# A transformer block on one core: the front before K reordered (single x loads, a shared PSUM bank, the scale through a row of ones), and the shift section and the s store moved

## The chip, the cores and the metric

The kernel runs on one core of a Trainium2 chip. The metric is the device time of one execution in microseconds (us); for one core that is the core's own time. All times of stages below come from one profiled execution and count from the start of its span.

## The reference, cut to what matters

Two batches of 256 tokens, width 1152 (9 chunks of 128), 2 heads, an MLP of width 4608, all in bf16. The first part, which the change concerns, is the adaptive LayerNorm before K, Q and V:

```
mod = (silu(c) @ w_mod).reshape(B, 6, 1, D)
shift_a, scale_a, gate_a, shift_m, scale_m, gate_m = [mod[:, i] for i in range(6)]
h = layernorm(x) * (1 + scale_a) + shift_a
q, k, v = split(h @ wqkv)
attn = softmax(q @ k^T * Dh**-0.5)
x = x + gate_a * ((attn @ v) @ wo)
h2 = layernorm(x) * (1 + scale_m) + shift_m
return x + gate_m * (gelu(h2 @ w_fc1) @ w_fc2)
```

## The kernel before, in words

Tokens lie as four tiles of 128 (tiles 0, 1 are batch 0; tiles 2, 3 batch 1). The stages run in this order: LayerNorm 1 and K, then Q, scores and softmax, V, attention times V, the output projection with LayerNorm 2, and the two MLP products. On each engine the instructions run in the order in which the program is written: a loop at the end of the kernel ties every instruction to the one before it on its engine. Waits between engines are put in by the tile framework, which also hands out the banks: `aux` tiles have two PSUM banks, `acc` tiles six. A transposed block `pt`, a scale group `pm`, and the shift section `pn` are `aux` tiles; the K sums `pk` are `acc` tiles.

The front, line by line:

- L83 to L85 load c (on ScalarE's queue) and x (on SP's queue, one load per batch). L103 to L110 put w_scale_a and w_k on the same queue in four groups of chunks (0-1, 2-3, 4-5, 6-8): a group's scale columns, then its rows of w_k, the first six column tiles of K (KM1 = 6) at first and the last three afterwards. w_shift_a, w_q and the s_b loads (L476) follow on that queue.
- L169 are matmuls on zeros that keep TensorE running while nothing has landed. L172, L173 transpose c and form s = silu(c), kept as sT.
- `stats_piece` (L185) takes the statistics of a third of a tile on VectorE and closes them after the third; tile 1's statistics are taken on ScalarE (`act_stats`, L200) and closed by three small VectorE operations (`act_stats_finish`, L205). `sqrt1` (L216) is ScalarE's square root, `recip1` (L219) VectorE's reciprocal, `norm1` (L226) normalizes columns of a tile; the first 512 columns (CUT) of each tile come first, the rest after L381.
- `scale_group` (L241) forms 1 + scale_a of a group: 9 small matmuls per chunk with weights from w_scale_a, and a copy that adds one (L254 on VectorE, L256 on ScalarE).
- `transpose_x` (L260) transposes chunks of normalized tiles on TensorE into a bank, and `modulate` (L267) scales them into hT0 on VectorE ("d") or ScalarE ("a"). `modulated_transpose` (L275) does both for one chunk of all four tiles.
- `k_step` (L282) adds one chunk's product to the six K sums, for a range of tokens. L329 to L405 write out by hand how these pieces interleave. The six sums are evacuated (L407), `k_panel` (L312) makes the last three column tiles of K one by one, and `vec_section` (L412) forms the shift with small matmuls and one VectorE transpose.
- L434 to L442 add the shift: hT = hT0 + shift_a, on VectorE and ScalarE. Q (L493) reads hT.
- L388, L389 write s by rows to DRAM: one VectorE transpose and four DMA issues on POOL's queue. s_b (L476) reads it back, for scale_m's products on VectorE (L469).

Of the kernel before, what the change touches and what calls it, by code (L numbers as in the profile page):

```python
# [8 lines left out]
FP32 = mybir.dt.float32  # L9
BF16 = mybir.dt.bfloat16  # L10
ACT = mybir.ActivationFunctionType
# [8 lines left out]
def kernel(  # L20
# [11 lines left out]
    nc = tc.nc  # L32
    B, N, D = x.shape
# [3 lines left out]
    P = 128  # L37
    T = B * N
    NT = T // P
    TPB = N // P  # L40
    KD = D // P
# [3 lines left out]
    NPD = D // PW  # L45
# [6 lines left out]
    const = ctx.enter_context(tc.tile_pool(name="const", bufs=1))  # L52
# [18 lines left out]
    wmod_v = w_mod.rearrange("(k p) n -> p k n", p=P)  # L71
# [3 lines left out]
    S_SHIFT_A, S_SCALE_A, S_GATE_A, S_SHIFT_M, S_SCALE_M, S_GATE_M = range(6)  # L75
# [5 lines left out]
    x_sb = act.tile([P, NT, D], BF16, name="x_sb", tag="x_in")  # L81
    c_sb = act.tile([B * KD, P], BF16, name="c_sb")
    nc.scalar.dma_start(c_sb[:], c_v)  # L83
    for b in range(B):
        nc.sync.dma_start(x_sb[:, b * TPB:(b + 1) * TPB, :], x_v[:, b, :, :])  # L85

    zeros = const.tile([P, T], BF16, name="zeros")
    nc.vector.memset(zeros[:], 0.0)
    ident = const.tile([P, P], BF16, name="ident")
    make_identity(nc, ident[:])  # L90
    eps_t = const.tile([P, 1], FP32, name="eps_t")
    nc.vector.memset(eps_t[:], LN_EPS)  # L92
    one_t = const.tile([P, 1], FP32, name="one_t")
    nc.vector.memset(one_t[:], 1.0)
    SW = 32
    sT = act.tile([P, KD, SW], BF16, name="sT")
    nc.gpsimd.memset(sT[:], 0.0)
# [5 lines left out]
    for k0, k1 in KGROUPS:  # L103
        nc.sync.dma_start(
            w_scale_a[:, :, k0 * P:k1 * P],
            wmod_v[:, :, S_SCALE_A * D + k0 * P:S_SCALE_A * D + k1 * P],
        )
# [92 lines left out]
    def act_stats(f, dst):  # L200
        nc.scalar.activation(
            xns[T_ACT][:], x_sb[:, T_ACT, :], f, bias=pivot, scale=-1.0, accum_out=dst[:],
        )
# [12 lines left out]
    def sqrt1(t):  # L216
        nc.scalar.activation(rstd1[:, t:t + 1], mv1[:, t, 1:2], ACT.Sqrt, bias=eps_t[:], scale=1.0)
# [20 lines left out]

    scale_a = act.tile([P, KD, B], FP32, name="scale_a")

    def scale_group(g):  # L241
        k0, k1 = KGROUPS[g]
        pm = aux_tile([P, k1 - k0, B], "pm")
        for j in range(k0, k1):
            for k in range(KD):
                nc.tensor.matmul(
                    pm[:, j - k0, :], w_scale_a[:, k, j * P:(j + 1) * P], sT[:, k, 0:B],
                    start=(k == 0), stop=(k == KD - 1),
                )

        def add_one(eng):
            dst = scale_a[:, k0:k1, :]
            if eng == "d":
                nc.vector.tensor_scalar_add(dst, pm[:], 1.0)  # L254
            else:
                nc.scalar.activation(dst, pm[:], ACT.Identity, bias=one_t[:])  # L256

        return add_one

    def transpose_x(ks, ts, pt=None, js=None):  # L260
        pt = aux_tile([P, len(ks), len(ts) * P], "pt", BF16) if pt is None else pt
        for i, k in enumerate(ks):
            for j, t in enumerate(ts) if js is None else zip(js, ts):
                nc.tensor.transpose(pt[:, i, j * P:(j + 1) * P], xns[t][:, k * P:(k + 1) * P], ident[:])
        return pt

    def modulate(pt, i, k, t0, j0, w, eng):  # L267
        b = t0 // TPB
        dst, src, sc = hT0[:, k, t0 * P:t0 * P + w], pt[:, i, j0:j0 + w], scale_a[:, k, b:b + 1]
        if eng == "d":  # L270
            nc.vector.tensor_scalar_mul(dst, src, sc)
        else:
            nc.scalar.mul(dst, src, sc)
# [8 lines left out]
    def k_step(k, c0=0, c1=T):  # L282
        for m in range(KM1):
            if k == 0 and c0 == 0:
                pk[m] = acc_tile([P, T], "pk")
            nc.tensor.matmul(  # L286
                pk[m][:, c0:c1], w_k[:, k, m * P:(m + 1) * P], hT0[:, k, c0:c1],
                start=(k == 0 and c0 == 0), stop=(k == KD - 1), skip_group_check=True,
            )
# [19 lines left out]
    def k_evac(m):  # L309
        evac(kT[:, m, :], pk[m][:])  # L310

    def k_panel(m):  # L312
        pk[m] = acc_tile([P, T], "pk")
        for k in range(KD):
# [12 lines left out]

    CUT = 4 * P
    warm(12, pwarm)  # L329
    act_stats(ACT.Identity, dsum)  # L330
    for j in range(NPD):
        stats_piece(0, j)
    sqrt1(0)
    act_stats(ACT.Square, dsq)
    stats_piece(2, 0)
    recip1(0)
    norm1(0, 0, CUT, "d")
    stats_piece(2, 1)
    pt_0 = transpose_x([0, 1], [0])
    warm(4, pwarm)  # L340
    act_stats_finish()
    sqrt1(T_ACT)
    stats_piece(2, 2, False)
    recip1(1)
    norm1(1, 0, CUT, "d")
    stats_aggregate(2)
    scale_group(0)("a")
    for k in range(2):
        modulate(pt_0, k, k, 0, 0, P, "a")
    warm(1, pwarm)  # L350
    pt_1 = transpose_x([0, 1], [1])
    for k in range(2):
        modulate(pt_1, k, k, 1, 0, P, "d")
    sqrt1(2)
    k_step(0, 0, P)
    k_step(1, 0, P)
    stats_piece(3, 0)
    recip1(2)
    norm1(2, 0, CUT, "d")
    k_step(0, P, N)  # L360
    k_step(1, P, N)
    stats_piece(3, 1)
    stats_piece(3, 2)
    pt_2 = transpose_x([0, 1], [2])
    for k in range(2):
        modulate(pt_2, k, k, 2, 0, P, "a")
    scale_group(1)("a")
    sqrt1(3)
    recip1(3)
    norm1(3, 0, CUT, "d")  # L370
    k_step(0, N, N + P)
    k_step(1, N, N + P)
    pt_3 = transpose_x([2, 3], [0, 1])
    for i, k in enumerate((2, 3)):
        modulate(pt_3, i, k, 0, 0, N, "a")
    pt_4 = transpose_x([0, 1], [3])
    for k in range(2):
        modulate(pt_4, k, k, 3, 0, P, "d")
    k_step(2, 0, N)
    k_step(3, 0, N)  # L380
    norm1(0, CUT, D, "d")  # L381
    norm1(1, CUT, D, "d")
    pt_5 = transpose_x([2, 3], [2, 3])
# [1 line left out]
        modulate(pt_5, i, k, 2, 0, N, "a")  # L385
    norm1(2, CUT, D, "d")
    norm1(3, CUT, D, "d")
    nc.vector.transpose(s_rows[:].rearrange("p k c -> p (k c)"), sT[:].rearrange("p k c -> p (k c)"))  # L388
    store_by_quadrant(s_dram[:].rearrange("b (k a r) -> a b k r", a=4, r=32), s_rows, B)  # L389
    k_step(0, N + P, T)  # L390
    k_step(1, N + P, T)
    scale_group(2)("d")
    k_step(2, N, T)
    modulated_transpose(4)
    k_step(3, N, T)
    modulated_transpose(5)
# [508 lines left out]
```

## Time and profile before, and how to read it

| what | us |
|---|---|
| median of 8 runs | 243.6 (243.49 to 244.08) |
| the profiled execution's own time | 243.94 |
| its span | 242.2 |
| x of batch 0, of batch 1 landed | 4.34, 5.8 |
| scale groups 0, 1, 2, 3 landed | 8.86, 11.92, 15.0, 19.0 |
| first k_step starts | 10.22 |
| k_step of chunk 2 starts | 14.13 |
| last piece of w_shift_a landed | 30.8 |
| shift section starts | 30.34 |
| Q starts | 33.51 |
| first MLP product starts | 97.4 |

In the tables by stretches the columns are: the stretch, its length, then busy time (and instructions) of TensorE's matmuls, its weight loads, VectorE, ScalarE and GpSimd, then the granted TensorE clock, the mean busy share of the 16 DMA engines, and GB/s. In a timeline, a line is start, duration, engine, source line, operation, output from input, shape and count; in brackets stands how long the engine had been idle before it and what ended that. Ends of matmuls are modelled, and a matmul that runs in a stream overlaps the next: the spacing of starts is the cost, not the duration. A landing time is the start of a load's issue plus the profile's time from issue to landing.

### The profile page before, as it was taken

The page shows a single profiled execution, that of the slowest core. Times are in us where ns is not written, and L with a number is a line of the kernel's source. Part 1 is how long each engine was busy: PE and PEld are TensorE (multiplying, and loading weights), DVE is VectorE, ACT ScalarE, POOL GpSimd, SP SyncE. Part 2 cuts the span into 40 slices and gives each one's busy share as a digit, 9 for nine tenths or more (in the row PEclk, how much of TensorE's full clock was granted, in tenths as well). Part 3 has the DMA queues.
Part 4 walks back from the last instruction along what each step waited for, and adds up shares of the span by engine and source line. Part 5 has one row for each costly group of instructions (what it writes and reads, how often), then busy time and mean ns, then how long its engine had stood idle before and what let it go on. Part 6 is the DMA issues. An engine that isn't in the chain of part 4 may idle for free.

```text
span 242.2 us, 4031 instructions
## 1 busy us (share of the span) xinstructions
PE 236.2 (98%) x1698; PEld 143.0 (59%) x1698; DVE 93.2 (38%) x207; ACT 70.4 (29%) x140; POOL 31.9 (13%) x48
## 2 busy tenths in 40 slices
PE   8899999999999999999999999999999999999994
PEld 2586454466566566888854444444656665665573
DVE  3762450665694676620000019999002000000001
ACT  6542250543736073782222233332000000000000
POOL 1022000000310617200000000000314111111111
PEclk9999999999999999999999999999999999999999
DMA  6999999999999999899999999997791000000000
GB/s 227 325 333 342 385 355 240 337 369 284 237 323 361 381 259 193 223 195 328 327 326 262 196 249 329 326 327 218 230 297 42 19 16 16 20 19 27 21 16 16
DMA packets 76989, 54.48 MB, mean 225 GB/s; under 512 B 26011, under 2 KB 72491, under 8 KB 76971
## 3 DMA queue, kind: packets, MB, share of 16 engines
q1 hardware_dynamic: 76240, 53.02, 78.0%
q0 software_dynamic: 704, 1.20, 1.6%
q8 instruction: 13, 0.21, 0.4%
q14 instruction: 5, 0.04, 0.1%
q10 hardware_dynamic: 27, 0.00, 0.0%
HBM read 46.90 MB, written 1.19 MB: 199 GB/s over the span
## 4 chain that ended last, share of the span: by engine, by line
PE 58%; ACT 2%; DMA 2%; issue 0%; DVE 0%; ACTq 0%; DVEq 0%
PE pacc L850 29%; PE pacc L786 29%; ACT hT L671 2%; DMA hT<-xn 2%; ACT xn L650 0%; ACT rstd L641 0%; DVE tmp L856 0%; DVE o_sb L858 0%; ACTq L671 0%; DVEq L856 0%
## 5 line engine op out<-in xcount | busy, mean ns | idle before, releaser
L786 PE MATMUL pacc<-hT,w_f 128*128 128x256 bf16 (+1 forms) x432 | 70.7, 326 | 0.3 <-ACT hT L671 0.2
L850 PE MATMUL pacc<-w_f,gT 128*128 128x384 bf16 (+2 forms) x468 | 70.5, 314 | 0.0
L850 PEld LDWEIGHTS <-gT 128*128 128x128 bf16 x468 | 44.4, 98 | 26.2
L786 PEld LDWEIGHTS <-w_f 128*128 128x128 bf16 x432 | 42.2, 98 | 28.3 <-issue 0.7
L469 DVE SCALAR_TENSOR_TENSOR late<-w_gate_mT,late 128x1152 bf16<-128x1152 bf16 x18 | 24.4, 1358 | 36.7 <-DMA w_gate_mT<-in_w_mod_dram 36.1
L856 DVE TENSOR_TENSOR tmp<-pacc,gate 128x384 f32<-128x384 f32 (+2 forms) x13 | 6.8, 526 | 62.2 <-PE pacc L850 50.4
L824 ACT ACTIVATE gT<-pacc 128x512 bf16<-128x512 f32 x24 | 14.3, 597 | 32.3 <-PE pacc L786 32.3
L469 DVE SCALAR_TENSOR_TENSOR s_spill<-w_scale_m,s_b 128x1152 bf16<-128x1152 bf16 x12 | 16.3, 1357 | 8.6 <-DMA w_scale_m<-in_w_mod_dram 8.3
L689 PE MATMUL pacc<-w_o,big 128*128 128x384 bf16 (+2 forms) x117 | 17.9, 314 | 0.0
L568 PE MATMUL pacc<-w_v,hT 128*128 128x384 bf16 x108 | 17.9, 326 | 0.0
L858 POOL TENSOR_TENSOR o_sb<-tmp,x 128x384 bf16<-128x384 f32 (+1 forms) x12 | 11.6, 973 | 47.1 <-DVE tmp L856 47.1
L689 PEld LDWEIGHTS <-big 128*128 128x128 bf16 x117 | 11.0, 98 | 6.8 <-ACT big L611 0.2
L568 PEld LDWEIGHTS <-hT 128*128 128x128 bf16 x108 | 10.4, 98 | 7.0 <-issue 0.2
L286 PE MATMUL pk<-big,w_k 128*128 128x128 bf16 (+2 forms) x102 | 13.4, 278 | 0.1
L695 POOL TENSOR_TENSOR x<-tmp,x_sb 128x384 f32<-128x384 f32 (+1 forms) x11 | 9.8, 889 | 17.4 <-DVE tmp L694 9.9
L495 PE MATMUL pacc<-hT,w_q 128*128 128x512 bf16 x54 | 11.8, 379 | 0.0
L324 POOL DMA_DIRECT2D gates_dram<-grow x4 | 2.1, 518 | 71.0 <-DVE grow L810 71.0
L802 ACT ACTIVATE gT<-pacc 128x512 bf16<-128x512 f32 x12 | 6.9, 595 | 10.2 <-PE pacc L786 10.2
L286 PEld LDWEIGHTS <-w_k 128*128 128x128 bf16 x102 | 7.8, 97 | 3.1 <-issue 0.2
L495 PEld LDWEIGHTS <-w_q 128*128 128x128 bf16 x54 | 5.3, 98 | 6.4
L694 DVE TENSOR_TENSOR tmp<-pacc,gate 128x384 f32<-128x384 f32 (+2 forms) x13 | 6.7, 522 | 5.4 <-PE pacc L689 5.2
L169 PE MATMUL pwarm<-zeros 128*128 128x512 bf16 x21 | 7.6, 515 | 1.2 <-DVE eps_t L92 1.2
(99 smaller groups left out, 159.6 us busy)
## 6 DMA issues: line engine op xcount, KB each, us to landing
w_f<-in_w_fc_dram SPq DMA_DIRECT2D x14, 864.0 KB, 10.8
w_f<-in_w_fc_dram SPq DMA_DIRECT2D x2, 2592.0 KB, 10.5
w_f<-in_w_fc_dram SPq DMA_DIRECT2D x2, 1728.0 KB, 14.2
w_shift_a<-in_w_mod_dram SPq DMA_DIRECT2D x3, 864.0 KB, 11.0
w_v<-in_wqkv_dram SPq DMA_DIRECT2D x3, 864.0 KB, 6.1
w_gate_a<-in_w_mod_dram SPq DMA_DIRECT2D x3, 864.0 KB, 9.2
w_o<-in_wo_dram SPq DMA_DIRECT2D x3, 864.0 KB, 6.4
w_shift_m<-in_w_mod_dram SPq DMA_DIRECT2D x3, 864.0 KB, 13.0
```

Source lines behind the costliest of these rows:

```text
L169: nc.tensor.matmul(dst[:], zeros[:, 0:P], zeros[:], start=True, stop=True)
L286: nc.tensor.matmul(pk[m][:, c0:c1], w_k[:, k, m * P:(m + 1) * P], hT0[:, k, c0:c1], start=(k == 0 and c0 == 0), stop=(k == KD - 1), skip_g ...
L469: nc.vector.scalar_tensor_tensor(spill, wT[:, j, :], 1.0, s_b[b], op0=ALU.mult, op1=ALU.mult, accum_out=dst(j, b),)
L495: nc.tensor.matmul(pq[m][:], w_q[:, k, m * P:(m + 1) * P], hT[:, k, :], start=(k == 0), stop=(k == KD - 1),)
L568: nc.tensor.matmul(pacc[:], hT[:, k, t * P:(t + 1) * P], w_v[:, k, pnl * PW:(pnl + 1) * PW], start=(k == 0), stop=(k == KD - 1),)
L689: nc.tensor.matmul(pacc[:], aT[:, k, t * P:(t + 1) * P], w_o[:, k, c0:c1], start=(k == ks[0]), stop=(k == ks[-1]),)
L695: (nc.vector if (t, i) in ((1, 2), (3, 3)) else nc.gpsimd).tensor_tensor(x1[:, t, c0:c1], tmp[:], x_sb[:, t, c0:c1], op=ALU.add)
L786: nc.tensor.matmul(dst, w_f1[m // KD][:, k, ml * P:(ml + 1) * P], hT[:, k, c0:c1], start=(k == 0), stop=(k == KD - 1),)
L802: nc.scalar.activation(gT[:, ms[0]:ms[-1] + 1, b * N:(b + 1) * N], pacc[:], ACT.Gelu_apprx_tanh)
L824: nc.scalar.activation(gT[:, m, :], pacc[:], ACT.Gelu_apprx_tanh)
L850: nc.tensor.matmul(pacc[:], gT[:, kk, t * P:(t + 1) * P], w_f2[j][:, r, c0 - n * PW:c0 - n * PW + cw], start=(kk == 0), stop=(kk == KF - 1),)
L858: (nc.vector if last else nc.gpsimd).tensor_tensor(o_sb[:], tmp[:], x1[:, t, c0:c0 + cw], op=ALU.add)
```

## The change

- x of batch 0 is loaded as two single tiles, batch 1 as before in one load.
- The constant one is now a row of 128 ones in bf16 on a single partition. A scale group starts with one matmul of that row by itself, which puts 1 into the bank; the 9 matmuls per chunk add to it, and the copy that follows adds nothing.
- For chunks 0, 1 of tile 0 and chunks 2, 3 of tiles 0, 1, VectorE scales straight with the scale in PSUM; ScalarE's copy to scale_a follows.
- Tile 1's and 2's chunks 0, 1 and the chunks 2, 3 of tiles 0, 1 are transposed into one bank (pt_1), eight blocks of 128 columns.
- VectorE's order changes: all three pieces of tile 2 and the first of tile 3 come ahead of tile 1's reciprocal and norm.
- `k_step` can do some of its six column tiles: chunk 3's step is split around tile 3's transposes, chunk 5's around scale group 3. Scale group 2 moves ahead of the k_steps of chunks 0, 1 for tile 3; its copy stays after them.
- The shift section moves into the last K tile: 5 of its 9 matmuls, the section, then 4.
- The s transpose and its four stores move behind chunk 8's scaling.

```diff
-    for b in range(B):
-        nc.sync.dma_start(x_sb[:, b * TPB:(b + 1) * TPB, :], x_v[:, b, :, :])
+    for l in range(TPB):
+        nc.sync.dma_start(x_sb[:, l, :], x_v[:, 0, l, :])
+    nc.sync.dma_start(x_sb[:, TPB:NT, :], x_v[:, 1, :, :])
...
+    def scale_group_matmuls(g):
         k0, k1 = KGROUPS[g]
         pm = aux_tile([P, k1 - k0, B], "pm")
+        nc.tensor.matmul(
+            pm[:].rearrange("p j b -> p (j b)"), ones_r[:, 0:P], ones_r[:, 0:(k1 - k0) * B], start=True, stop=False,
+            skip_group_check=True,
+        )
...
-                    start=(k == 0), stop=(k == KD - 1),
+                    start=False, stop=(k == KD - 1), skip_group_check=True,
...
-    act_stats(ACT.Identity, dsum)
     for j in range(NPD):
         stats_piece(0, j)
+    act_stats(ACT.Identity, dsum)
     sqrt1(0)
     act_stats(ACT.Square, dsq)
-    stats_piece(2, 0)
     recip1(0)
     norm1(0, 0, CUT, "d")
-    stats_piece(2, 1)
+    for j in range(NPD):
+        stats_piece(2, j)
     pt_0 = transpose_x([0, 1], [0])
     warm(4, pwarm)
     act_stats_finish()
     sqrt1(T_ACT)
-    stats_piece(2, 2, False)
+    sqrt1(2)
+    stats_piece(3, 0)
     recip1(1)
     norm1(1, 0, CUT, "d")
-    stats_aggregate(2)
-    scale_group(0)("a")
+    pm_0 = scale_group_matmuls(0)
     for k in range(2):
-        modulate(pt_0, k, k, 0, 0, P, "a")
-    warm(1, pwarm)
-    pt_1 = transpose_x([0, 1], [1])
+        nc.vector.tensor_scalar_mul(hT0[:, k, 0:P], pt_0[:, k, 0:P], pm_0[:, k, 0:1])
+    nc.scalar.copy(scale_a[:, 0:2, :], pm_0[:])
+    pt_1 = aux_tile([P, 1, 8 * P], "pt", BF16)
...
     for k in range(2):
-        modulate(pt_1, k, k, 1, 0, P, "d")
-    sqrt1(2)
+        transpose_into(pt_1, k, k, 1)
+    recip1(2)
+    norm1(2, 0, CUT, "d")
+    for k in range(2):
+        modulate(pt_1, 0, k, 1, k * P, P, "a")
     k_step(0, 0, P)
     k_step(1, 0, P)
-    stats_piece(3, 0)
-    recip1(2)
-    norm1(2, 0, CUT, "d")
-    k_step(0, P, N)
-    k_step(1, P, N)
     stats_piece(3, 1)
     stats_piece(3, 2)
-    pt_2 = transpose_x([0, 1], [2])
     for k in range(2):
-        modulate(pt_2, k, k, 2, 0, P, "a")
-    scale_group(1)("a")
+        transpose_into(pt_1, 6 + k, k, 2)
+    k_step(0, P, N)
+    for k in (2, 3):
+        for t in range(TPB):
+            transpose_into(pt_1, 2 * (k - 1) + t, k, t)
+    k_step(1, P, N)
+    for k in range(2):
+        modulate(pt_1, 0, k, 2, (6 + k) * P, P, "a")
     sqrt1(3)
+    k_step(0, N, N + P)
+    pm_1 = scale_group_matmuls(1)
     recip1(3)
     norm1(3, 0, CUT, "d")
-    k_step(0, N, N + P)
+    for k in (2, 3):
+        nc.vector.tensor_scalar_mul(
+            hT0[:, k, 0:N], pt_1[:, 0, 2 * (k - 1) * P:2 * k * P], pm_1[:, k - 2, 0:1]
+        )
+    nc.scalar.copy(scale_a[:, 2:4, :], pm_1[:])
     k_step(1, N, N + P)
-    pt_3 = transpose_x([2, 3], [0, 1])
-    for i, k in enumerate((2, 3)):
-        modulate(pt_3, i, k, 0, 0, N, "a")
+    k_step(2, 0, N)
+    k_step(3, 0, N, 0, 3)
     pt_4 = transpose_x([0, 1], [3])
     for k in range(2):
         modulate(pt_4, k, k, 3, 0, P, "d")
-    k_step(2, 0, N)
-    k_step(3, 0, N)
+    k_step(3, 0, N, 3, KM1)
...
-    nc.vector.transpose(s_rows[:].rearrange("p k c -> p (k c)"), sT[:].rearrange("p k c -> p (k c)"))
-    store_by_quadrant(s_dram[:].rearrange("b (k a r) -> a b k r", a=4, r=32), s_rows, B)
+    add2 = scale_group(2)
     k_step(0, N + P, T)
     k_step(1, N + P, T)
-    scale_group(2)("d")
+    add2("d")
...
     k_step(4)
+    k_step(5, m1=2)
     scale_group(3)("d")
     modulated_transpose(6)
-    k_step(5)
+    k_step(5, m0=2)
     modulated_transpose(7)
     k_step(6)
     modulated_transpose(8)
+    nc.vector.transpose(s_rows[:].rearrange("p k c -> p (k c)"), sT[:].rearrange("p k c -> p (k c)"))
+    store_by_quadrant(s_dram[:].rearrange("b (k a r) -> a b k r", a=4, r=32), s_rows, B)
...
     k_evac(7)
+    k_panel(8, 0, 5)
     shift_a = vec_section(sT, w_shift_a, "shift_a")
-    k_panel(8)
+    k_panel(8, 5)
```

More of the change, by code (lines that the diff above doesn't have):

```diff
@@ L92 @@
     nc.vector.memset(eps_t[:], LN_EPS)
-    one_t = const.tile([P, 1], FP32, name="one_t")
-    nc.vector.memset(one_t[:], 1.0)
+    ones_r = const.tile([1, P], BF16, name="ones_r")
+    nc.vector.memset(ones_r[:], 1.0)
     SW = 32
@@ L102, with load_scale_group @@
     w_k = wide_tile("w_k")
[L103 to L107, printed above, removed]
+    def load_scale_group(g, eng):
+        c0, c1 = KGROUPS[g][0] * P, KGROUPS[g][1] * P
+        eng.dma_start(w_scale_a[:, :, c0:c1], wmod_v[:, :, S_SCALE_A * D + c0:S_SCALE_A * D + c1])
+    for g, (k0, k1) in enumerate(KGROUPS):
+        load_scale_group(g, nc.sync)
         for k in range(k0, k1):
@@ L239 @@
     scale_a = act.tile([P, KD, B], FP32, name="scale_a")
-    def scale_group(g):
+    def scale_group_matmuls(g):
         k0, k1 = KGROUPS[g]
         pm = aux_tile([P, k1 - k0, B], "pm")
+        nc.tensor.matmul(
+            pm[:].rearrange("p j b -> p (j b)"), ones_r[:, 0:P], ones_r[:, 0:(k1 - k0) * B], start=True, stop=False,
+            skip_group_check=True,
+        )
         for j in range(k0, k1):
@@ L247, in scale_group, with scale_group_copy, copy_out @@
                     pm[:, j - k0, :], w_scale_a[:, k, j * P:(j + 1) * P], sT[:, k, 0:B],
-                    start=(k == 0), stop=(k == KD - 1),
+                    start=False, stop=(k == KD - 1), skip_group_check=True,
                 )
-        def add_one(eng):
+        return pm
+    def scale_group_copy(g, pm):
+        k0, k1 = KGROUPS[g]
+        def copy_out(eng):
             dst = scale_a[:, k0:k1, :]
             if eng == "d":
-                nc.vector.tensor_scalar_add(dst, pm[:], 1.0)
+                nc.vector.tensor_copy(dst, pm[:])
             else:
-                nc.scalar.activation(dst, pm[:], ACT.Identity, bias=one_t[:])
-        return add_one
+                nc.scalar.copy(dst, pm[:])
+        return copy_out
+    def scale_group(g):
+        return scale_group_copy(g, scale_group_matmuls(g))
     def transpose_x(ks, ts, pt=None, js=None):
@@ L280, with k_step @@
     pk = [None] * KD
-    def k_step(k, c0=0, c1=T):
-        for m in range(KM1):
+    def k_step(k, c0=0, c1=T, m0=0, m1=KM1):
+        for m in range(m0, m1):
             if k == 0 and c0 == 0:
@@ L310, in k_evac, with k_panel @@
         evac(kT[:, m, :], pk[m][:])
-    def k_panel(m):
-        pk[m] = acc_tile([P, T], "pk")
-        for k in range(KD):
+    def k_panel(m, ka=0, kb=KD):
+        if ka == 0:
+            pk[m] = acc_tile([P, T], "pk")
+        for k in range(ka, kb):
             nc.tensor.matmul(
@@ L342, with transpose_into @@
     sqrt1(T_ACT)
-    stats_piece(2, 2, False)
+    sqrt1(2)
+    stats_piece(3, 0)
     recip1(1)
     norm1(1, 0, CUT, "d")
-    stats_aggregate(2)
-    scale_group(0)("a")
+    pm_0 = scale_group_matmuls(0)
     for k in range(2):
-        modulate(pt_0, k, k, 0, 0, P, "a")
-    warm(1, pwarm)
-    pt_1 = transpose_x([0, 1], [1])
-    for k in range(2):
-        modulate(pt_1, k, k, 1, 0, P, "d")
-    sqrt1(2)
+        nc.vector.tensor_scalar_mul(hT0[:, k, 0:P], pt_0[:, k, 0:P], pm_0[:, k, 0:1])
+    nc.scalar.copy(scale_a[:, 0:2, :], pm_0[:])
+    pt_1 = aux_tile([P, 1, 8 * P], "pt", BF16)
+    def transpose_into(pt, slot, k, t):
+        nc.tensor.transpose(pt[:, 0, slot * P:(slot + 1) * P], xns[t][:, k * P:(k + 1) * P], ident[:])
+    for k in range(2):
+        transpose_into(pt_1, k, k, 1)
[3 more added lines that the diff above has]
+        modulate(pt_1, 0, k, 1, k * P, P, "a")
     k_step(0, 0, P)
     k_step(1, 0, P)
-    stats_piece(3, 0)
-    recip1(2)
-    norm1(2, 0, CUT, "d")
-    k_step(0, P, N)
-    k_step(1, P, N)
     stats_piece(3, 1)
     stats_piece(3, 2)
-    pt_2 = transpose_x([0, 1], [2])
     for k in range(2):
-        modulate(pt_2, k, k, 2, 0, P, "a")
-    scale_group(1)("a")
+        transpose_into(pt_1, 6 + k, k, 2)
[6 more added lines that the diff above has]
+        modulate(pt_1, 0, k, 2, (6 + k) * P, P, "a")
     sqrt1(3)
+    k_step(0, N, N + P)
+    pm_1 = scale_group_matmuls(1)
     recip1(3)
     norm1(3, 0, CUT, "d")
-    k_step(0, N, N + P)
+    for k in (2, 3):
[3 more added lines that the diff above has]
+    nc.scalar.copy(scale_a[:, 2:4, :], pm_1[:])
     k_step(1, N, N + P)
-    pt_3 = transpose_x([2, 3], [0, 1])
-    for i, k in enumerate((2, 3)):
-        modulate(pt_3, i, k, 0, 0, N, "a")
+    k_step(2, 0, N)
+    k_step(3, 0, N, 0, 3)
     pt_4 = transpose_x([0, 1], [3])
```

## The prediction

> **What bounds the kernel now.** I read the page first, then the chain that ended last, then the timeline of the first 34 us, since the change lies there.
>
> ```profile
> PE 236.2 (98%) x1698; PEld 143.0 (59%) x1698; DVE 93.2 (38%) x207; ACT 70.4 (29%) x140; POOL 31.9 (13%) x48
> ```
>
> TensorE is never free for long. The chain of waits, in order of time, ends in two stretches of nothing but matmuls:
>
> ```profile
> 98.87 69.59 PE pacc L786 x425
> 168.46 70.30 PE pacc L850 x468
> ```
>
> No TensorE wait of over 0.3 us stands between 14.13 us and 98.87 us, and what starts that last chain (LN2) is itself fed by TensorE. So a shift of the front reaches the end in full. The table by stretches says where the front has room:
>
> ```profile
> 8.86:10.22 1.36, 1.12 (x22) 0.72 (x23) 0.29 (x3) 0.68 (x3) 0.00 (x0) 1.00 1.15 321
> 10.22:14.13 3.91, 3.53 (x62) 2.97 (x62) 3.14 (x10) 2.04 (x8) 0.00 (x0) 1.00 1.13 320
> 14.13:33.51 19.38, 19.38 (x200) 11.83 (x198) 8.38 (x24) 6.29 (x15) 2.58 (x4) 1.00 1.07 360
> ```
>
> From 14.13 us on TensorE is dense. Before that the timeline has the steps:
>
> ```profile
> 4.98 1.24 ACT L201 ACTIVATE xn<-x_sb 128x1152 bf16<-128x1152 bf16 x1
> 6.21 0.28 ACT L217 ACTIVATE rstd<-mv,eps_t 128x1 f32<-128x1 f32 x1
> 8.86 0.60 PE L246 MATMUL pm<-sT,w_scale_a 128*128 128x2 bf16 x18 [0.42 <-DMA w_scale_a<-in_w_mod_dram]
> 9.50 0.26 ACT L256 ACTIVATE scale_a<-pm,one_t 128x4 f32<-128x4 f32 x1 [1.24 <-PE pm L246]
> 9.80 0.62 ACT L273 ACTIVATE big<-pt,scale_a 128x128 bf16<-128x128 bf16 x2
> 9.82 0.27 PE L264 MATMUL pt<-ident,xn 128*128 128x128 bf16 x2
> 10.22 1.50 PE L286 MATMUL pk<-big,w_k 128*128 128x128 bf16 x24
> 13.61 0.84 ACT L273 ACTIVATE big<-pt,scale_a 128x256 bf16<-128x256 bf16 x2 [0.42 <-PE pt L264]
> 14.13 1.47 PE L286 MATMUL pk<-big,w_k 128*128 128x256 bf16 x12
> ```
>
> k_step starts at 10.22 us. Its 36 narrow matmuls at 0.055, 8 transposes at 0.055 and 18 scale matmuls at 0.027 make 2.9 us of issue until 14.13, so about 1.0 us is waiting: that is all that the front could give.
>
> **What the skill says.** (1) "PSUM — Partial Sum Buffer", PSUM bank collisions raise a hardware error: two engines may not touch one bank and quadrant at once, so software orders them. The trace agrees: chunk 4's transposes run from 17.44 to 17.83, and its first scaling starts only at 17.86, though it reads the first two; and pt_1's transposes, placed in the bank of the first pm, start at 9.82, after ScalarE's last read of it at 9.76. (2) "TensorEngine Tiling (Array Packing)", Tiling Modes, Key Properties: changing the tiling mode drains TensorE. The trace agrees: before 64-row matmuls the weight load stood idle, and the first one comes 0.20 us after its forerunner (54.38 to 54.58) where 0.11 is the spacing, thus 0.09 more; the 18-row transpose at 3.02 is followed by a 128-row matmul at 3.14.
>
> ```profile
> 54.58 0.33 PEld L532 LDWEIGHTS <-big 64*128 64x128 bf16 x8 [0.21 <-issue]
> 30.34 0.98 PEld L417 LDWEIGHTS <-sT 128*32 128x32 bf16 x36 [0.42 <-issue]
> ```
>
> **The change, part by part.**
>
> *Loads.* SP issues three loads of x for two, at 0.43 us each, so the first scale group is issued 0.43 later. DMA share is 0.8 to 1.1 from 2.5 us on, so a load queued 0.43 later may still be served at once when its turn comes; I expect its landing (8.86) to move by 0 to 0.43. Tile 0 may land some 0.7 earlier than 4.34. That gives nothing: the square root of tile 0 (6.21) stands in ScalarE's queue behind the statistics of tile 1 (4.98), which stand behind a table load; the order of these two is not changed.
>
> *VectorE's new order.* Spacings from the trace, start to start: reciprocal 0.20, half norm 0.32, a statistics piece 0.47 (0.58 before its aggregate), aggregate 0.16, 128-wide scaling 0.20 (0.28 long). Reciprocal 6.53, norm 6.73 as before; then three pieces of tile 2 (7.05), aggregate 8.57, the three closing sums of tile 1 (8.73, 8.91, 8.98), a piece of tile 3 (9.05), reciprocal 9.52 and norm 9.72 of tile 1 (8.57 before), the two scalings of pt_0 10.05 and 10.25, ending 10.53. The queue waits for nothing on the way: the old order filled the wait for the square root with a piece of tile 2, the new one leaves that time empty and does 0.94 us more ahead of tile 1's norm. Scaling straight from pm saves ScalarE's 0.26 + 0.36 but comes 0.25 us after the old one (9.80).
>
> *TensorE behind it.* pt_1 needs an aux bank; both are read by the second scaling (pt_0 and pm_0), so its transposes start at 10.58 and k_step(0) at 10.69, 0.47 late. The group's slack of 0.55 (ready 9.50, used 10.05) covers the later load. Then: ScalarE scales tile 1 10.90 to 11.52; tile 2's transposes go into the same bank, after that, 11.56; k_step half, four transposes of chunks 2, 3, k_step half, to 12.55; ScalarE may read the bank after the four (12.39), so tile 2's first chunk is ready at 12.79; k_step 12.84 to 13.17. Group 1 landed at 11.92, cover 1.2 us.
>
> *The row of ones.* One more matmul per scale group, with one row for 128. If it takes the 32-row mode it costs 0.1 going in and 0.12 coming out, 0.22; if not, 0.03. Neither is shown for one row; I take 0.22. In group 0 it lies before the wait for the load. In group 1 it is on the path: pm_1 ends 14.02, VectorE's 256-wide scaling (0.346) gives chunk 2 at 14.41, k_step(2) starts 14.45 against 14.13, with tile 3's two transposes (0.11) still to do: **+0.43**. That PSUM scalars are read by VectorE is not in the trace; 0 to 0.1 each for two on the path, taken as 0.
>
> *Group 2 moved ahead of two k_steps.* It needs a bank: pt_4's is free once VectorE has scaled both chunks, 0.80 after its first transpose, and TensorE is there after 0.66 (2 + 4 transposes, 3 matmuls of 0.11): 0.19 stalled with the 0.05 of signalling, and 0.12 to leave the mode: **+0.31**. In the old order 12 matmuls (0.67) were between. The other bank would be ready 0.9 later; that is the high end, 0 the low.
>
> *Group 3 inside k_step(5)*: the row, **+0.22**; its load landed at 19.0, TensorE comes after 20.9. The four matmuls of 0.216 and chunk 7's transposes cover the scaling of chunk 6, so no wait.
>
> *K's last tile split.* After the shift section the old order has 9 matmuls of 0.2165 (1.95); w_q could start at 32.72 (VectorE's second add starts 32.39, 0.28 long, 0.05) and starts at 33.51: slack 0.79. The new order leaves 4, 1.08 less cover: **+0.29**. What it hides, a late w_shift_a (last piece 30.77, needed about 31.0), did not stall.
>
> *s store.* The transpose (0.47) leaves VectorE at 16.03 and runs behind chunk 8's scaling, about 26.0; its four DMA issues on POOL (2.58) end near 29, landing 5.5 after the last issue: near 34. SP holds the s_b loads till then (32.1 before for the second), and the transposing load, w_v and w_gate_a behind it. The DMA backlog (w_q's last piece lands at 38.1) hides it; VectorE's products end at 52.6 and the softmax starts at 55.01: 2.4 us of cover. Taken as 0; 0.8 if the cover is gone.
>
> Sum: 0.43 + 0.31 + 0.22 + 0.29 = **1.25 us**. The profiled execution took 243.94 (span 242.2 and 1.7 around it) and lies 0.34 above the median: 245.19 for it, 243.6 + 1.25 = **244.85** for the median.
>
> **Rivals.** *Cheap row, free bank (within 0.2%).* If the ones keep the 128-row mode (0.48 less), reads and writes of different slots of pt_1 are not ordered (0.3 less) and pm_2 finds a bank (0.19 less), 0.28 is left: 243.9. For it: no one-row matmul is in the trace; against it, 18 rows and 64 rows both paid.
>
> *The front is filled (faster).* One mechanism: VectorE is in time, so k_step starts at 10.22 and runs through the new transposes and pieces without the 1.0 us of waits, to 13.2 for 14.13: 0.82 gained with pt_4 left; the early front also covers the bank and the shift, and cheap ones cost 0.08 to 0.2: 242.9 to 243.0. It decides from k_step(2) before 13.5. Against it: VectorE's queue is full from 6.53 to 10.5 by its own durations.
>
> *s is late (slower still).* SP falls over 0.7 us further behind than TensorE does, which is w_o's cover (last panel lands 79.0, needed 79.7): up to 0.8 more, 245.65. Against it: SP waits for the softmax at about 65 and catches up there.
>
> **How the numbers follow.** Forecast 0.64 (244.85, its own range 244.3 to 245.4), cheap row 0.16, filled front 0.08, late s 0.12. A measurement tells 0.2%, 0.49 us, from no change. Slower by more: 0.64 + 0.12 = 0.76; within: 0.16; faster: 0.08. The range goes down to the cheap row (243.8) and up to late s with a PSUM scalar's 0.1 (245.75).
>
> **What would show it.** k_step(0) at 10.7 behind a second scaling that ends at 10.5; k_step(2) at 14.4 or 14.5; a 0.2 hole in the weight loads at each row of ones; a bank wait ahead of group 2; w_q beginning behind the second shift add, not behind the last K matmul, at about 34.76; the end later by the same. Wrong: k_step(0) before 10.3, spacing at the ones of 0.03, or w_q's start and the end moving by different amounts.

## The result, and the profile after

The changed kernel takes **245.91 us** in the median of 11 executions (245.15 to 247.9), against 243.82 in 32 executions of the kernel before beside it (243.35 to 244.58). The ratio over all executions (not of the two medians) is 1.0095, with a 95% interval of 1.0079 to 1.0111. A twelfth execution of the changed kernel is on record with 244.67; it is in neither figure. The kernel is slower, as forecast, but by 2.1 us where 1.25 was forecast, and just outside the range (up to 245.75). The profiled execution took 245.62 (span 243.8).

The chain of waits of the changed kernel, in order of time (start, length, what), begins with another piece than my steps did, a load of x:

```profile
1.66 6.35 DMA x_sb<-in_x_dram
8.03 1.49 DVE stats L189 x3
...
99.86 70.35 PE pacc L816 x432
170.21 70.31 PE pacc L880 x468
```

L816 is the first MLP product (L786 before, from 98.87), L880 the second (L850, from 168.46); the second starts 1.75 us later than before. The timeline of the changed kernel has the front, step by step:

```profile
1.66 0.43 SPq L86 DMA_DIRECT2D x_sb<-in_x_dram  x1
2.14 0.43 SPq L107 DMA_DIRECT2D w_scale_a<-in_w_mod_dram  x1
8.03 1.48 DVE L189 BATCH_NORM_STATS2 stats<-x_sb 128x6 f32<-128x384 bf16 x3 [0.90 <-DMA x_sb<-in_x_dram]
10.04 0.60 PE L253 MATMUL pm<-sT,w_scale_a 128*128 128x2 bf16 x18 [1.14 <-DMA w_scale_a<-in_w_mod_dram]
11.03 0.48 DVE L365 TENSOR_SCALAR big<-pt,pm 128x128 bf16<-128x128 bf16 x2
11.56 0.27 PE L370 MATMUL pt<-ident,xn 128*128 128x128 bf16 x2 [0.93 <-DVE big L365]
11.67 0.83 PE L301 MATMUL pk<-big,w_k 128*128 128x128 bf16 x12
```

Batch 1, issued 0.46 us later, lands 2.2 us later: at 8.0, where it was 5.8. Scale group 0 lands at 10.0, 1.2 late. VectorE, whose statistics of tile 2 I put at 7.05, starts them at 8.03. From there each step runs by the forecast's own durations: 11.03 for 10.05, 11.56 for 10.58, 11.67 for 10.69.

The tables by stretches, first of the kernel before and then of the changed one, are cut at the same events: k_step(0), k_step(2), the last K tiles, Q.

```profile
10.22:14.13 3.91, 3.53 (x62) 2.97 (x62) 3.14 (x10) 2.04 (x8) 0.00 (x0) 1.00 1.13 320
14.13:26.36 12.23, 12.23 (x137) 8.40 (x135) 5.32 (x17) 3.49 (x9) 2.58 (x4) 1.00 1.08 350
26.36:33.51 7.15, 7.15 (x65) 3.43 (x63) 3.05 (x8) 2.80 (x7) 0.00 (x0) 1.00 1.06 378
```

```profile
11.67:15.48 3.81, 3.50 (x64) 3.01 (x62) 2.51 (x8) 1.52 (x6) 0.00 (x0) 1.00 1.11 320
15.48:28.31 12.83, 12.81 (x139) 8.63 (x139) 5.43 (x18) 3.33 (x9) 1.08 (x2) 1.00 1.08 362
28.31:35.76 7.45, 7.32 (x64) 3.43 (x63) 2.72 (x7) 2.02 (x5) 1.49 (x3) 1.00 1.07 353
```

| stretch | forecast | measured |
|---|---|---|
| up to k_step(0) | +0.47 | +1.45 (11.67 for 10.22) |
| k_step(0) to k_step(2) | -0.15 | -0.10 (3.81 for 3.91) |
| k_step(2) to the last K tiles: two transposes, groups 2 and 3 | +0.64 | +0.60 (12.83 for 12.23) |
| the last K tiles, up to Q | +0.29 | +0.30 (7.45 for 7.15) |
| Q later by | +1.25 | +2.25 (35.76 for 33.51) |
| span longer by | +1.25 | +1.6 |

(The 0.11 of tile 3's two transposes, which my sum had in the front's 0.43, stands in the third row here.) So all but 0.02 of the excess of 1.00 at Q is in the first row, and at the end of the kernel 0.65 of the 2.25 is missing. The experiments ask for the cause of the first and of the second.

### The profile page after: what moved, and what is told of

Read it like the earlier page. It is cut to its first block, busy times and chain, and to the rows that moved or that the text cites. A ratio compares the mean times of both kernels' runs of the same rounds, so it can differ in the third digit from the quotient of the medians.

```text
span 243.8 us, 4041 instructions
## 1 busy us (share of the span) xinstructions
PE 236.8 (97%) x1701; PEld 143.4 (59%) x1701; DVE 93.8 (38%) x209; ACT 69.2 (28%) x138; POOL 31.9 (13%) x48
## 4 chain that ended last, share of the span: by engine, by line
PE 93%; DMA 3%; DVE 2%; ACT 0%; SPq 0%; issue 0%; DVEq 0%; ACTq 0%
PE pacc L816 29%; PE pacc L880 29%; PE pacc L719 7%; PE pacc L598 7%; PE pacc L525 5%; PE pk L301 4%; DMA x_sb<-in_x_dram 3%; PE pacc L533 2%; PE pk L331 2%; PE pa L633 1%; PE ps_s L553 1%; PE pn L446 1%; DVE stats L189 1%; PE pm L253 1%; PE pt L279 1%; PE pg L481 0%
## 5 line engine op out<-in xcount | busy, mean ns | idle before, releaser
L816 PE MATMUL pacc<-hT,w_f 128*128 128x256 bf16 (+1 forms) x432 | 70.5, 326 | 0.0
L880 PE MATMUL pacc<-w_f,gT 128*128 128x384 bf16 (+2 forms) x468 | 70.5, 314 | 0.0
L880 PEld LDWEIGHTS <-gT 128*128 128x128 bf16 x468 | 44.4, 98 | 26.2
L816 PEld LDWEIGHTS <-w_f 128*128 128x128 bf16 x432 | 42.2, 98 | 27.8 <-issue 0.2
## 6 DMA issues: line engine op xcount, KB each, us to landing
w_f<-in_w_fc_dram SPq DMA_DIRECT2D x14, 864.0 KB, 11.3
```

The costliest lines, as they stand in the source:

```text
L816: nc.tensor.matmul(dst, w_f1[m // KD][:, k, ml * P:(ml + 1) * P], hT[:, k, c0:c1], start=(k == 0), stop=(k == KD - 1),)
L880: nc.tensor.matmul(pacc[:], gT[:, kk, t * P:(t + 1) * P], w_f2[j][:, r, c0 - n * PW:c0 - n * PW + cw], start=(kk == 0), stop=(kk == KF - 1),)
```

## The experiments

Theory: dividing batch 0's load is what delays batch 1, and with it VectorE's whole order. Rivals: VectorE's order or the PSUM scalars cost more than I took them for; or the later issue as such delays the loads. The kernel before, run beside each group of experiments, has medians of 243.75 to 243.80; ratios and intervals are again over all executions.

**One part undone: x by two loads.**

```diff
-    for l in range(TPB):
-        nc.sync.dma_start(x_sb[:, l, :], x_v[:, 0, l, :])
-    nc.sync.dma_start(x_sb[:, TPB:NT, :], x_v[:, 1, :, :])
+    for b in range(B):
+        nc.sync.dma_start(x_sb[:, b * TPB:(b + 1) * TPB, :], x_v[:, b, :, :])
```

> The changed kernel with x loaded by two loads again, one per batch; all else as changed. Theory L (the loads): the 1.0 us by which k_step(2) came later than forecast (15.48 for 14.45) is VectorE waiting for batch 1's x, which landed at 8.0 instead of 5.8. Expected: batch 1 lands at 5.8, the three pieces of tile 2 start at 7.05, pt_0's second scaling ends near 10.5, k_step(2) starts near 14.45, Q starts near 34.8; the end 0.5 to 1.0 us earlier than the changed kernel, since the LayerNorm 2 hand-over takes part of a shift. Rival O (the order alone): VectorE's new order and the bank waits make the whole delay and the load's landing only fell into time that was lost anyway: k_step(2) stays at 15.3 to 15.5 and Q at 35.6 or more.

Measured: 245.64 in the median of four (245.79, 245.83, 245.49, 244.83), 1.0072 times (1.0048 to 1.0095). Two lines of its timeline:

```profile
7.14 1.47 DVE L188 BATCH_NORM_STATS2 stats<-x_sb 128x6 f32<-128x384 bf16 x3
10.78 0.83 PE L300 MATMUL pk<-big,w_k 128*128 128x128 bf16 x12
```

The statistics no longer wait, and k_step(0) is at 10.78, 0.09 from the forecast. Yet the profiled execution reaches Q at 35.84, as late as the changed kernel, and the median is only 0.27 below it, where 0.5 to 1.0 was expected. The table by stretches says why: the last but two column, the granted TensorE clock, is at half from 11.75 to 15.0 us. I call this a fall of the clock from here on.

```profile
11.75:15.00 3.25, 3.25 (x44) 3.04 (x44) 1.12 (x4) 0.81 (x3) 0.00 (x0) 0.51 1.12 324
```

3.25 us at half the clock lower the mean clock of the span to 0.993; 0.992 is measured. Three of these four executions have a mean of 0.992 or 0.993, and the one that has not (0.999) took 244.83, what my sum of steps gave (244.85).

**That part alone, in the kernel before.** The same three loads as in the changed kernel, nothing else.

> The kernel before with only the load of batch 0 split into single tiles. Theory L: batch 1 lands near 8.0 and scale group 0 near 10.0, as in the changed kernel. Tile 2's first piece stands ahead of tile 0's reciprocal in the old order, so the norms move by some 2 us and k_step starts at 11.3 to 12 for 10.22; Q 1 to 1.5 us later, the end 0.5 to 1.5 later. Rival D (only the issue is 0.43 later): batch 1 lands at 6.2, group 0 at 9.3, k_step starts near 10.65, the end moves by less than 0.5.

Measured: 245.71 of seven, 1.0068 times (1.0047 to 1.0089); its timeline has

```profile
8.58 0.56 DVE L187 BATCH_NORM_STATS2 stats<-x_sb 128x6 f32<-128x384 bf16 x1 [3.16 <-DMA x_sb<-in_x_dram]
```

Batch 1 lands late here too (8.55; scale group 0 at 10.5), so the delay comes with the loads alone. In the old order this statistics piece stands ahead of tile 0's reciprocal, so the delay costs more here: k_step(0) is at 12.57, later than the 11.3 to 12 expected, with the last 2.4 us of that at half the clock. The clock fell (0.50 from 10.2 to 13.5) in three of seven executions; the other four have a median of 244.97.

**Two more parts, each undone beside x.** First the row of ones as a 128-row matmul, then the shift section ahead of all nine matmuls:

```diff
-    ones_r = const.tile([1, P], BF16, name="ones_r")
+    ones_r = const.tile([P, 8], BF16, name="ones_r")
...
-            pm[:].rearrange("p j b -> p (j b)"), ones_r[:, 0:P], ones_r[:, 0:(k1 - k0) * B], start=True, stop=False,
+            pm[:].rearrange("p j b -> p (j b)"), ident[:], ones_r[:, 0:(k1 - k0) * B], start=True, stop=False,
...
-    k_panel(8, 0, 5)
     shift_a = vec_section(sT, w_shift_a, "shift_a")
-    k_panel(8, 5)
+    k_panel(8)
```

> x by two loads, and the row of ones made by a full-height matmul (the identity times 128 rows of ones), so TensorE keeps its 128-row mode. Theory M (mode change, 0.2 us for each row on the path): group 1's first scale matmul comes 0.2 earlier after its k_step, group 2 saves 0.1, group 3 saves 0.2: Q starts 0.5 us earlier than with x by two loads alone (near 34.3). Rival N (no mode cost for one row): under 0.1 us.

> x by two loads, and the shift section ahead of all nine matmuls of K's last tile again. Theory S: Q waits for the second shift add in the changed order; with nine matmuls behind the section the wait of 0.29 us goes, and Q follows the last K matmul: Q starts 0.3 us earlier than with x by two loads alone (near 34.5). Rival W: w_shift_a's last piece lands late and the section itself waits, so nothing is won.

Measured: 244.52 (1.0034, interval 1.0017 to 1.005) and 244.48 (1.0045, 1.0024 to 1.0065). Where the clock held, the medians are 244.25 (seven of eleven) and 244.42 (seven of twelve), with 244.83 for x alone (one execution). Both profiles have the fall, so Q (35.36 and 35.32) is not at the 34.3 and 34.5 expected, and the terms are read by stage: from the row of group 2 to the last K tiles 10.75 us with the identity and 11.01 without, so 0.26 for the modes of groups 2 and 3; the last K tiles 7.15 us with the section ahead (28.17 to 35.32), 0.30 less. Both terms are near the size forecast (0.12 + 0.22, of which the 128-row matmuls keep 0.03 each; and 0.29). In both kernels the executions in which the clock fell take about 0.95 us more than the others.

**Is it idle TensorE that makes the clock fall?** The first kernel of this section with 10 more matmuls on zeros in TensorE's waits:

```diff
-    warm(12, pwarm)
+    warm(14, pwarm)
...
-    warm(4, pwarm)
+    warm(7, pwarm)
...
     pm_0 = scale_group_matmuls(0)
+    warm(5, pwarm)
```

> The changed kernel with x by two loads, as in the first run of this study, and 10 more matmuls on zeros (2 ahead of the first two transposes, 3 ahead of scale group 0's matmuls, 5 between these and the second pt_1 transposes), each 0.216 us from start to start, all in time in which TensorE stood idle. Theory (idle TensorE in the front lets the granted clock fall to 0.5 for some 3.3 us in some executions): no execution shows the fall, all lie near 244.8, those of the upper group at 245.5 to 245.8 are gone. Rival (the fall comes from load that follows, or from chance, and not from idle TensorE): the two groups stay, 244.8 and 245.7, and the median with them.

Measured: 245.31 in the median of four (245.06, 245.56, 245.07, 245.73), 1.0069 times (1.0054 to 1.0085). The mean clock is never under 0.998, so in none of the four did it fall. The level was missed: the filling itself holds group 0's matmuls to 9.42 and k_step(0) to 11.07, 0.29 later than without, and 0.5 between the executions remains with another cause.

**Does a shift of the front reach the end?** The kernel before with `warm(1)` made `warm(6)`.

> The kernel before with warm(1) ahead of the pt_1 transposes made warm(6): five matmuls of 0.216 us more, so that k_step(0) starts some 0.8 us later (the transposes waited for VectorE until 9.82 and now come at 10.64), with TensorE never idle. My prediction took a shift of the front to reach the end in full: +0.8, 244.6. Theory now (the wait at LN2's hand-over, 0.6 us before and gone after, takes the later shares back): the shift is +0.8 at the Q stage, and the span grows by 0.2 to 0.4 only, 244.0 to 244.2.

Measured: 244.35 of nine, 1.0026 times (1.0016 to 1.0036). Q is at 34.35, +0.84; the span grew by 0.3 and the median by 0.55, between the two expectations. The wait at LN2's hand-over (the first matmuls of the first MLP product waiting for LayerNorm 2's output) is gone here, but not because TensorE is late, as the last part of this section shows.

**Late issue, or division?** Two more kernels from the one before: a load of 128 bytes between the two loads of x, and batch 1 divided instead of batch 0.

```diff
+    nc.sync.dma_start(idle_x[:], x_v[0:1, 0, 0, 0:64])
```

```diff
-        nc.sync.dma_start(x_sb[:, b * TPB:(b + 1) * TPB, :], x_v[:, b, :, :])
+    nc.sync.dma_start(x_sb[:, 0:TPB, :], x_v[:, 0, :, :])
+    for l in range(TPB):
+        nc.sync.dma_start(x_sb[:, TPB + l, :], x_v[:, 1, l, :])
```

> The kernel before with one load of 128 bytes, read by nobody, between batch 0's load and batch 1's on SP: batch 1 and all later loads are issued some 0.43 us later, and no load is divided. Theory (the later issue costs only itself, the division is what costs): batch 1 lands at 6.2 to 6.3, group 0 at 9.3; 243.9 to 244.2. Rival (what made batch 1 land at 8.0 is the issue behind the weights of the other queues, or the third load as such): batch 1 lands at 7.5 to 8.5 and the time is 245.0 or more.

> The kernel before with batch 0 by one load and batch 1 by two, one for each tile: the same three loads and the same issue times for all that follows as in the changed kernel, the division put on the other batch. Theory (a load for one tile takes 2304-byte pieces where a load for two takes 4608, and the pieces of the tiles hold up what is queued behind them): batch 0 lands at 4.3, tile 2 before 6.3, tile 3 and group 0 some 0.5 to 1.2 late (group 0 at 9.4 to 10.0); 244.2 to 245.0. Rival (only a whole load behind single ones is overtaken): tile 2 by 5.8 and group 0 at 9.3, time within 0.3 of before, 243.8 to 244.1.

Measured: 244.22 (1.0025, 1.0007 to 1.0042) and 244.37 (1.0029, 1.0015 to 1.0042). The pieces of tile 2 in the two timelines, without a wait for x in either:

```profile
6.01 0.56 DVE L188 BATCH_NORM_STATS2 stats<-x_sb 128x6 f32<-128x384 bf16 x1
```

```profile
6.02 0.50 DVE L187 BATCH_NORM_STATS2 stats<-x_sb 128x6 f32<-128x384 bf16 x1
```

Group 0 is used at 8.72 and 8.89, against 8.86 before: neither the later issue nor a third load delays anything in the front, and k_step(0) starts at 10.07 and 10.25. What the small load costs appears elsewhere: in its profile TensorE waits 0.44 us for w_shift_a, the last of a row of loads that are all issued later. With batch 1 divided, the clock fell in 3 of 20 executions, and the other 17 have a median of 244.22. The time of 244.37 is in the range of the theory (244.2 to 245.0), but the late landings from which that came are absent: tile 2 landed at 5.0, tile 3 at 6.2, group 0 at 8.9. What the other 0.4 is, these runs don't show.

**All four tiles singly,** in the kernel before:

> The kernel before with x by four loads, one for each tile of both batches. Theory (single loads for batch 0's tiles come first and hold up what follows them, whatever its form): tile 2 lands at 6.5 to 8.5, group 0 at 9.7 to 10.5; 244.6 to 245.6. Rival (only a whole load that stands behind single ones is held up; it lands behind group 0's first bytes): tile 2 lands by 5.8 as with batch 1 alone divided, group 0 at 9.3, and the time is 243.9 to 244.4.

Measured: 244.68 of 22, 1.003 times (1.0019 to 1.0041).

```profile
6.07 0.56 DVE L187 BATCH_NORM_STATS2 stats<-x_sb 128x6 f32<-128x384 bf16 x1 [0.69 <-DMA x_sb<-in_x_dram]
```

The rival holds for the loads, nearly: tile 2 has landed by 6.07, group 0 at 9.4. So of the divisions only one delays x by 2 us: a load for two tiles that stands behind loads for one. All three profiles of that form show it (8.0, 8.55, and 8.6 below). It is not the only thing that moves the landing: in the profile with the identity, batch 1 stands behind a whole load and still landed at 7.2, where 5.8 to 6.0 is the rule; there VectorE reached it at 7.19, so it cost next to nothing. The time, 244.68, is in the theory's range, because the clock fell in 5 of 22; the median of the other 17 is 244.34, in the rival's.

**The filling on the changed kernel itself, and the parts together.** First the changed kernel with 6 more matmuls on zeros (2 ahead of group 0's, 4 behind them); then the same filling with x by two loads, the identity and the shift section taken back; then with groups 2 and 3 in their old places as well.

```diff
-    add2 = scale_group(2)
     k_step(0, N + P, T)
     k_step(1, N + P, T)
-    add2("d")
+    scale_group(2)("d")
...
-    k_step(5, m1=2)
     scale_group(3)("d")
     modulated_transpose(6)
-    k_step(5, m0=2)
+    k_step(5)
```

> The changed kernel whole, with 6 matmuls on zeros more in TensorE's idle time (2 ahead of scale group 0's matmuls, 4 between these and the second pt_1 transposes). Theory (TensorE's idle time in the front makes the granted clock fall in about half of the executions): no execution has a mean clock under 0.995, and those of 246.5 and more are gone; median 245.2 to 245.7. Rival (the fall has another cause): the clock falls to 0.992 in about half, median 245.9.

> The changed kernel with three of its parts taken back at once: x by two loads, the row of ones by a 128-row matmul on the identity, the shift section ahead of all nine matmuls of K's last tile; and 6 matmuls on zeros more in TensorE's idle time (2 ahead of scale group 0's matmuls, 4 behind them). What stays is VectorE's new order, the shared bank, the scalings out of PSUM and groups 2 and 3 moved. Theory (the parts add up): x by two loads alone gave 244.83 where the clock held, the identity took 0.59 off that, the shift section 0.42: 243.8 to 244.0 and no execution of the upper group. Rival (with an earlier Q the waits of 0.2 to 0.9 at LN2's hand-over come back and take a part of it): 244.2 to 244.4.

> The kernel of e9_three_back with scale groups 2 and 3 put back to their old places as well (group 2 behind k_step(1), group 3 ahead of k_step(5)). Theory (the moved group 2 stands 0.19 behind its bank, and nothing is won by it): 0.1 to 0.3 less than e9_three_back, 243.6 to 243.9. Rival (the moved groups win the overlap of their copies, some 0.2 each): 0.2 to 0.4 more than e9_three_back, 244.1 to 244.4.

Measured, with the kernel before at 243.75 in 59 executions: the filled change 246.03 (1.0104, 1.0084 to 1.0124); three parts back 243.99 (1.0013, 1.0006 to 1.0021); four back 243.94 (1.0011, 1.0002 to 1.0019). The first is a miss: the clock fell in one of six, not in none, and the median is no lower. Its profile tells why:

```profile
8.65 1.48 DVE L189 BATCH_NORM_STATS2 stats<-x_sb 128x6 f32<-128x384 bf16 x3 [1.52 <-DMA x_sb<-in_x_dram]
```

```profile
10.64 0.60 PE L253 MATMUL pm<-sT,w_scale_a 128*128 128x2 bf16 x18 [1.56 <-DMA w_scale_a<-in_w_mod_dram]
```

Batch 1 lands later still, and TensorE is idle for 1.6 us whatever was put before that wait. Three parts back came as expected (243.8 to 244.0); four back, at 243.94, missed the 243.6 to 243.9 by little. The clock fell in none of the 44 executions of the two, and the three parts together, with the filling, account for 1.9 of the 2.1 us. Between groups 2 and 3 moved and in place, the profiles have 0.17 at Q:

```profile
34.03 3.19 PE L524 MATMUL pacc<-hT,w_q 128*128 128x512 bf16 x14
```

```profile
33.86 3.40 PE L522 MATMUL pacc<-hT,w_q 128*128 128x512 bf16 x15
```

That is the 0.19 of bank stall that I had put there: in place, 12 matmuls stand between pt_5's transposes and the row of group 2 (15.97 to 16.64) and cover the bank; moved, the row comes 0.41 after the first of four transposes (15.73 to 16.14), which take 0.22 to issue. The medians, 0.05 apart, don't tell the two kernels apart. No version beat the kernel before.

**Where 0.65 us went at the end.** From Q's start to the end, the spans of ten profiles agree within 0.2 us (208.04 for the changed kernel, 208.15 for the later front, 208.17 and 208.14 for three and four parts back). Before it was 208.69. The difference lies in waits between the first eight matmuls of the first MLP product: its first matmul starts 2.25 us later in the changed kernel (99.69 for 97.44), as Q does, but its eighth only 1.74 later (100.61 for 98.87). The timelines of ScalarE, before, changed and with the shift section back, show where that comes from (in brackets, how long ScalarE had waited):

```profile
94.59 3.06 ACT L671 ACTIVATE hT<-hT,shift_m,scale_m 128x256 bf16<-128x256 bf16 x6 [3.93 <-DMA hT<-xn]
```

```profile
96.33 3.06 ACT L701 ACTIVATE hT<-hT,shift_m,scale_m 128x256 bf16<-128x256 bf16 x6 [3.41 <-DMA hT<-xn]
```

```profile
97.10 3.06 ACT L699 ACTIVATE hT<-hT,shift_m,scale_m 128x256 bf16<-128x256 bf16 x6 [4.62 <-DVE tmp L722]
```

The transposing load of hT that comes here, the second of four, took 3.3 us from issue to landing in the profile of the changed kernel, 3.8 in that of the one before and 4.5 in the third (where the profile names VectorE, which ended just after the landing). It isn't lateness that removes the wait: Q is at 33.86 with four parts back, and ScalarE's wait is short (3.41) and TensorE has none; Q is at 35.32 with the shift section back, and the load is long and TensorE waits 0.9. Why the load is long in four of the fourteen profiles isn't settled by these runs.

## Why the prediction was right and wrong

**Right in direction and in most of its steps.** VectorE's order, its durations, the bank that both scalings must leave, the row's mode, the bank stall of group 2, the split of the last K tile (Q now starts behind the second shift add, at 35.76) and the s store, which costs nothing visible: each is in the trace with about the size I gave it. The PSUM scalars that I took at 0 cost 0: the two scalings take 0.48 together, as they do from SBUF.

**The step that failed is the one on the loads,** and the sentence that rests on it. I wrote that group 0's landing moves "by 0 to 0.43", said nothing of batch 1's, and then: "The queue waits for nothing on the way". Group 0 moved by 1.2, batch 1 by 2.2, and VectorE's queue waited 0.90 us for x, exactly where the new order puts all of tile 2's pieces ahead of tile 1's norm. This is 0.98 of the 1.0 us that Q lies beyond the forecast. I had costed the division at its issue time; two runs show that the issue time alone costs the front nothing, and the division of batch 0 alone reproduces the delay. The range shared the fault: its upper end, 245.75, was made of a late s and a PSUM scalar, of which neither came, and had no term for a late x.

The Trainium skill, "DMA: Bandwidth & Descriptors", Queues, rings and completion order, says that a load is spread over up to 16 rings and that loads of one issuing engine don't complete in the order of issue. The rates agree: when batch 1 landed, the kernel before had moved 227 GB/s x 5.8 us = 1.32 MB, of which x is 1.18; the changed one 220 x 8.0 = 1.76 MB. So 0.58 MB of later loads, for 0.14, had passed while part of batch 1 was still outstanding. Why a whole load falls behind after single ones, and single ones do not, no run shows.

**Not foreseen: the clock.** The new order leaves TensorE idle twice for about 1 us in the front (for group 0, then for VectorE's scalings, where the old order had a warm matmul). In 20 of 45 executions of the five kernels with such a front or such loads (the changed one 5 of 11) the granted clock then fell to half for some 3.4 us; of the kernel before, in one of the 120 whose clock is on record, and why in that one stays open. With TensorE's waits filled and x by two loads it fell in none of 48. Put in order by the waits of TensorE that the profile shows before 14.2 us, the kernels fall into three groups: up to 0.8 us in all, 1 fall in 189 executions; 1.2 and 1.6 us, 4 in 26; 1.7 to 2.1 us, 25 in 67. In the changed kernel the executions with the fall have a median of 246.8, those without 245.58, so it moves the median by about 0.3.

Why some executions of a kernel and not others, the traces suggest, though no run tested it by itself. In each of the fourteen profiles the clock changes only at whole multiples of 3.41 us from its first change on record, and these points lie elsewhere in each execution. (The first is the rise to full, at 4.5 to 7.4 us; before it the clock column says 1.00 too, but matmuls of 512 columns stand 0.43 us apart, for 0.2165 later.) In the first experiment the two longest waits lie between two such points, and the next stretch has half the clock. In the profiled execution of the changed kernel, which kept its clock, the two waits lie in two stretches (TensorE's busy time stands behind the length):

```profile
8.14:11.55 3.41, 1.89 (x35) 1.52 (x34) 3.19 (x15) 1.16 (x5) 0.00 (x0) 1.00 1.11 326
11.55:14.96 3.41, 3.31 (x45) 3.04 (x43) 1.32 (x5) 0.92 (x4) 0.00 (x0) 0.50 1.12 325
```

```profile
7.05:10.46 3.41, 2.27 (x28) 1.17 (x27) 2.37 (x9) 1.04 (x4) 0.00 (x0) 1.00 1.09 331
10.46:13.88 3.42, 2.29 (x40) 2.05 (x37) 2.66 (x10) 1.31 (x6) 0.00 (x0) 1.00 1.13 320
```

The five falls in the front follow stretches in which TensorE is idle for 1.3 to 2.0 us; no other stretch at the full clock up to 235 us has over 1.14. (An estimate that fits the ends of the kernels too counts matmuls by columns, at 0.42 ns each, from 0.2165 us for 512: stretches that stream for at most 0.38 of their time are followed by half the clock, and those with 0.44 or more are not.) The skill, "TensorE: Matmul & The Clock Gate", Part 1, gives an idle window of some 3.4 us as what halves the clock, counted in windows that run freely; its section "A second HAM failure mode: psum-queue depth-cycling" tells of falls through frequent short waits. The traces agree with the free windows and their length, but a window need not be idle throughout: the longest single wait ahead of the fall was 1.1 us in the first experiment and 2.0 in the second, and each fall in the profiles lasted one window.

**Wrong: "a shift of the front reaches the end in full".** 0.65 of it did not in the profiled pair, because the waits at the start of the first MLP product, which I had dismissed as under 0.3 us each (two, 0.12 and 0.22, by the profile), vary with a load, here by 0.5 us (2.25 less 1.74). They were in the kernel before's profile and not in the other's: the spans differ by 1.6 though Q differs by 2.25.

The sum, then, for the medians: 1.25 forecast, +1.0 for batch 1, about +0.3 for the clock, less some 0.45 that must be the share of the wait in the executions of before (2.09 measured). The last is what is left over, not measured by itself; the later front and three and four parts back, each with the short load in its profile, lost 0.29, 0.28 and 0.16 between Q and the median. That the miss is only 0.85 us is thus in part luck: two omissions of 1.3 us together were met by a loss in the kernel before that I had not counted.

**The rivals.** The cheap row and the free bank fell with the identity run (0.26 for two groups) and the bank stall. The filled front decided from k_step(2) before 13.5: it came at 15.48. A late s is not seen.

## What to carry to other kernels

Cost a changed load by what stands behind it in its queue, not by its own issue: ask for every later load when it lands and which engine's order begins with it. An order that puts all work on one input first turns a late landing one for one into time; one that mixes inputs may hide it, or, as with the division alone in the old order, may cost more. And when a reorder takes away matmuls on zeros, ask what they were keeping busy: two waits of 0.5 and 1.1 us close together were enough to lose half the clock for 3.4 us in some executions.

## What the runs showed of the hardware

- A load for two tiles issued behind two loads for one landed 6.3 to 7.0 us after its issue in three kernels; behind one load for two tiles it took 4.6 us in the kernel before, but 6.0 in one other profile; a tile of the same batch by itself, third in the queue, landed within 4.4 us.
- The granted clock halved for 3.41 us after stretches of 3.41 us in which TensorE was idle for 1.3 to 2.0 us, with single waits of no more than 1.1 us in four of five profiles. Executions of the same kernel differ in where these stretches begin.
- The second transposing load of hT landed 3.3 to 3.4 us after its issue in nine profiles, 3.8 in three and 4.5 in one.
